# Tiles of a chunked gated attention with a mixture of experts, laid out in multiples of 64 bytes

## The chip, the cores and the metric

The kernel runs on one core of a Trainium2 chip. The metric is the device time of one execution in microseconds (us), the median over several runs.

## The reference

Two parts, one after the other. The first is a gated linear attention: per head a 48 x 48 state is decayed by a gate row by row, takes in the outer product of k and v, and is read with q. The second gives the result to four experts, each of two matrix products with a ReLU between them, and adds their outputs weighted by normalised probabilities.

```python
# q, k, v, f_logit: (4, 8, 768, 48) float32
f = 1.0 / (1.0 + np.exp(-f_logit))
for t in range(S):
    state = f[:, :, t, :, None] * state + np.einsum('bhd,bhe->bhde', k[:, :, t], v[:, :, t])
    y[:, :, t] = np.einsum('bhd,bhde->bhe', q[:, :, t], state)
x = y.transpose(0, 2, 1, 3).reshape(3072, 384)
# domain_probs (3072, 4), w1 (4, 384, 1024), w2 (4, 1024, 384)
p = domain_probs / (domain_probs.sum(-1, keepdims=True) + 1e-09)
for e in range(4):
    h = np.maximum(x @ w1[e], 0.0)
    out += p[:, e:e + 1] * (h @ w2[e])
```

## The kernel before

The sequence of 768 positions is cut into six chunks of 128 (`C`, `T`). In a chunk the four batches (`B`) go through the attention one by one, positions on the partitions: the gate (L260, L264, on ACT), a cumulated sum on PE (L268), its exponentials (L288), the products of q and k with them (L296, on DVE or POOL), a transposition (on PE for the first batches, by a DMA transpose later), the scores (L320), their masking (L324, on DVE), the product with v (`pe_y`, L331 and L335), and the transposition of the result into `xT` (L360 on PE, or a DMA transpose). The state of a chunk is carried on in `Sf` and `Sb` (L348, L355, L356).

The experts work on the 512 rows of a chunk (four batches of 128): `mm_h` (L364) multiplies `w1` with `xT`, ReLU takes the result into `h` (L373 on DVE, L375 on ACT), `mm_o` (L379) multiplies `h` with `w2`, and `ev_o` (L386 to L390) weights it and adds it to `o`, which is stored (L394). For chunk 0 the experts begin with the rows of batches 0 and 1 (256 columns), then those of batches 2 and 3.

Inputs are loaded by SP (`load`, L232). A tile of `f`, `q`, `k` or `v` holds two batches; there are four tiles of each name, numbered by slots (f0 to f3). A row of a tile holds the heads one behind the other, 48 float32 each, so one load of one batch is 128 partitions x 8 pieces of 192 bytes, 192 KB. For chunk 0 each batch is loaded by itself, in this order:

```python
for i, x in enumerate("f0 k0 q0 f1 k1 q1 f2 f3 k2 q2 v0 k3 q3 v1 v2 v3".split()):
    add_load(0, x[0], int(x[1]), 1, -1000 + i)
```

The number here is the batch, not the slot: batches 0 and 1 go to the tiles of slot 0, batches 2 and 3 to those of slot 1. Between v of batch 0 and k of batch 3 stands the load of the probabilities (L247). The gate's load of chunk 1, batch 0, follows; later chunks are loaded in pairs of batches.

The weights are loaded by POOL (`load_w`, L239), cast from float32 to bfloat16 on the way, in eleven pieces: six of 768 KB read (`w1` of experts 0 and 1 and `w2` of expert 0, in halves), then five whole matrices. The first piece waits for the load of q of batch 3 in chunk 0, so that the weights do not take the transfers away from the first loads.

The order of all the work on each engine is fixed when the kernel is built: a planner (`Plan`) places every step by its priority, its dependences, its assumed cost on each engine and the number of slots of each tile. While PE has no expert work yet, matmuls on a constant tile (`busy`, L614) fill the gaps that the planner foresees.

Tiles are taken from three pools in on-chip memory: `const`, `wpool` and `wk`. A tile of `wk` gets its place when it is first used. Places follow one another, and every length is rounded up to a multiple of 32 bytes. Nearly all lengths are multiples of 64 bytes; `ones` (2 bytes in a partition), `ident32` and `psm` (96 each) and the eight `egs` (16 each) are not. In `const` only `pn` lies between `ident32` and `psm`, and the weights and `wk` come behind.

Of the kernel before, what the change touches and what calls it, by code (L numbers as in the profile page):

```python
# [8 lines left out]
FP32 = mybir.dt.float32  # L9
BF16 = mybir.dt.bfloat16  # L10
AF = mybir.ActivationFunctionType
# [91 lines left out]
def kernel(  # L103
# [11 lines left out]
    nc = tc.nc  # L115
    B, H, S, D = q.shape
    assert (B, H, S, D) == (4, 8, 768, 48)
    T = 128
    C = S // T
    HD = H * D  # L120
    NP = H // 2
    P2 = 64
    MP = P2 + D
# [9 lines left out]
    const = ctx.enter_context(tc.tile_pool(name="const", bufs=1))  # L133
# [15 lines left out]
    nc.gpsimd.tensor_copy(out=Ub, in_=U)  # L149
    ident = const.tile([T, T], BF16)  # L150
    make_identity(nc, ident)
    ones = const.tile([T, 1], BF16)
    nc.gpsimd.memset(ones, 1.0)
    pads = {}
    for nm, nb in (("gp", 2), ("qk", 2)):
# [3 lines left out]
    for i in range(rooms["e"]):  # L159
# [5 lines left out]
        out=mask01, in_=mask01, compare_op=ALU.is_ge, fill=0.0,  # L165
# [4 lines left out]
    Sb = []  # L170
# [3 lines left out]
        Sb.append(t)  # L174
    NR = B * C
    praw = const.tile([NR, T, E], FP32)
    ident32 = const.tile([NR, NR], FP32)
    nc.vector.tensor_copy(out=ident32, in_=ident[0:NR, 0:NR])
    pn = const.tile([T, E, NR], FP32)
    psm = const.tile([T, NR], FP32)  # L180
    w1_sb = wpool.tile([128, E, KD, F], BF16)
    w2_sb = wpool.tile([128, E, KF, Din], BF16)
    w1_r = moe_w1.rearrange("e (ko ki) f -> e ki ko f", ki=128)
# [3 lines left out]
    for nm, a in (("f", f_logit), ("q", q), ("k", k), ("v", v)):  # L187
# [2 lines left out]
    tiles = {}  # L190
    shapes = {
        "f": ([T, 2 * H, D], FP32), "q": ([T, 2 * H, D], FP32), "k": ([T, 2 * H, D], FP32), "v": ([T, 2 * H, D], FP32),
        "ex": ([T, 2 * H, D], FP32), "egs": ([128, NP], FP32), "vb": ([T, H, D], BF16),
        "QK": ([128, 2, NP, T], BF16), "AT": ([T, 2, NP, T], BF16), "yb": ([T, HD], BF16),
        "xT": ([128, KD, NT], BF16), "h": ([128, KF, NT], BF16), "o": ([128, Din], FP32),
        "cs": ([T, 512], FP32), "tp": ([128, 2, NP, T], BF16), "A": ([T, NP, T], FP32), "y": ([T, 512], FP32),
# [3 lines left out]
    def tl(kind, *key):  # L200

        if (kind, key) not in tiles:
            room = kind if kind in rooms else "ps_m" if kind in ("hp", "op", "pp") else "ps_t"
            slot = P.slot[(room, kind) + key if room.startswith("ps_") else (room,) + key]
            if room in ("gp", "qk", "e"):
                tiles[kind, key] = pads[room, slot]
            else:
                shape, dt = shapes[kind]
                pool = ps if room.startswith("ps_") else wk
                tiles[kind, key] = pool.tile(shape, dt, name=f"{room}{slot}")  # L210
        return tiles[kind, key]
# [61 lines left out]
    def e_part(c, b, j):  # L273

        e = tl("e", c, b)
        if j == 0 and c > 0:
            return e[:, 0:2 * NP * P2].rearrange("t (r d i) -> t i r d", r=2, i=NP)[:, :, :, 0:D]
        e = e[:, 2 * NP * P2:] if j else e[:, 0:HD]
        return e.rearrange("t (i r d) -> t i r d", d=D, r=2)

    def exps(c, b):
        cs = tl("cs", c, b)
        src = cs[:, 0:HD].rearrange("t (i r d) -> t i r d", r=2, d=D)
        for j in range(2):
            o, i = e_part(c, b, j), src
            if j == 0 and c > 0:
                o, i = (x.rearrange("t i r d -> t r i d") for x in (o, i))
            nc.scalar.activation(out=o, in_=i, func=AF.Exp, scale=1.0 if j else -1.0)  # L288
        if c == 0:
            nc.scalar.activation(out=tl("egs", c, b)[0:MP], in_=cs[0:MP, HD:HD + NP], func=AF.Exp, scale=-1.0)  # L290

    def dma_egs(c, b):
        nc.gpsimd.dma_start(out=tl("egs", c, b), in_=tl("e", c, b)[T - 1:T, 0:2 * NP * P2].rearrange("o (m i) -> o m i", i=NP))  # L293

    def product(c, b, j, eng):
        engines[eng].tensor_tensor(out=tl("qk", c, b)[:, j, :, 0:D].rearrange("t (i r) d -> t i r d", r=2),  # L296
# [51 lines left out]
            nc.vector.tensor_tensor(out=Sf[rows, b], in0=Sf[rows, b], in1=KV[rows, :, r, :], op=ALU.add)  # L348

    def state(c, b):  # L350
        egs, nb = tl("egs", c, b), Sb[(c + 1) % 2]
        for r in range(2):
            rows = slice(r * P2, r * P2 + D)
            eg = egs[rows, :].unsqueeze(2).broadcast_to([D, NP, D])
            nc.gpsimd.tensor_tensor(out=Sf[rows, b], in0=Sf[rows, b], in1=eg, op=ALU.mult)  # L355
            nc.gpsimd.tensor_copy(out=nb[rows, b, :, r * D:(r + 1) * D], in_=Sf[rows, b])  # L356
# [72 lines left out]
    def attention(c, slot, gran):  # L429
# [10 lines left out]
        for b in range(B):  # L440
# [5 lines left out]
            cs = P.add(f"cs {c}.{b}", {"PE": 0.17 if c else 0.36}, on(pe_cs), s(0),  # L446
                       deps=[G[b]], takes=[pt_("cs")], lag=0.2, frees=[("gp", c, half)])
            ex = P.add(f"exps {c}.{b}", {"ACT": 0.98 if c else 0.82}, on(exps), s(0) + 0.1, deps=[cs],
                       takes=[("e", c, b)] + ([("egs", c, b)] if c == 0 else []), frees=[pt_("cs")])
            GS.append(P.add(f"egs {c}.{b}", {"POOL": 0.8}, on(dma_egs), s(10), deps=[ex], takes=[("egs", c, b)],  # L450
                            frees=[("e", c, b)], lag=2.8) if c and more else None)
            pe = {"DVE": 0.47} if c == 0 and b == B - 1 else {"DVE": 0.47, "POOL": 1.36} if c == 0 else None
# [56 lines left out]
        for b in range(B if more else 0):  # L509
            on = lambda f, b=b: (lambda e: f(c, b))  # L510
            pt_ = lambda kind, b=b: ("ps_t", kind, c, b)
            s15 = slot(b, 15) if c else 2 + 2 * b
            kv = P.add(f"kv {c}.{b}", {"PE": 0.22}, on(pe_kv), s15, deps=[Y[b]] + (X[B - 1] if c == 0 else []),
                       takes=[pt_("KV")], frees=[("vb", c, b), ("qk", c, b)], lag=0.2)
            ek = P.add(f"ev_kv {c}.{b}", {"DVE": 0.74}, on(ev_kv), s15 + 0.1,
                       deps=[kv, kvdone.get((c - 1, b))], frees=[pt_("KV")])
            kvdone[c, b] = P.add(f"state {c}.{b}", {"POOL": 1.75}, on(state), s15 + 0.2,
                                 deps=[ek, GS[b]], frees=[("egs", c, b)])
# [130 lines left out]
```

## Time and profile before

| | |
|---|---|
| median of 5 runs | 300.46 us (300.15 to 301.05) |
| the profiled execution, its own time | 301.05 us |
| its span, first to last instruction | 299.3 us |
| PE busy (matmul) | 288.9 us, 97% |
| ACT, DVE, POOL busy | 176.4, 125.8, 105.5 us |
| read from HBM, written to it | 31.51 MB, 4.72 MB |
| packets of the queue that SP uses | 129348, 30.14 MB |

The page shows the span in 40 equal slices, one digit for each, in tenths of the slice that an engine was busy. PEclk is the share of TensorE's clock that was granted. The DMA line is the mean busy share of the 16 DMA engines. An answer about stretches of time gives, for each stretch, the busy time of each engine with the number of its instructions, the clock, the DMA share and the rate in GB/s. A line of the timeline gives start, length, engine, line and operation, and in brackets how long the engine was idle before and what ended that. The chain of waits is followed back from the last instruction: at each step to what released it.

### The profile page before, as it was taken

The page shows a single profiled execution, that of the slowest core. Times are in us where ns is not written, and L with a number is a line of the kernel's source. Part 1 is how long each engine was busy: PE and PEld are TensorE (multiplying, and loading weights), DVE is VectorE, ACT ScalarE, POOL GpSimd, SP SyncE. Part 2 cuts the span into 40 slices and gives each one's busy share as a digit, 9 for nine tenths or more (in the row PEclk, how much of TensorE's full clock was granted, in tenths as well). Part 3 has the DMA queues.
Part 4 walks back from the last instruction along what each step waited for, and adds up shares of the span by engine and source line. Part 5 has one row for each costly group of instructions (what it writes and reads, how often), then busy time and mean ns, then how long its engine had stood idle before and what let it go on. Part 6 is the DMA issues. An engine that isn't in the chain of part 4 may idle for free.

```text
span 299.3 us, 5544 instructions
## 1 busy us (share of the span) xinstructions
PE 288.9 (97%) x2132; PEld 171.5 (57%) x2160; DVE 125.8 (42%) x247; ACT 176.4 (59%) x325; POOL 105.5 (35%) x179
## 2 busy tenths in 40 slices
PE   6879999999999999999999999999999999999995
PEld 2448555577777776455555555555555555555554
DVE  6656003486576475027374454433442322201223
ACT  4766672857766677876464665554465544475440
POOL 5376501229389159325538554234220000000000
PEclk9998999999999999999999999999999999999999
DMA  9999999996999999999999962102442100200003
GB/s 144 195 190 204 208 208 206 193 153 166 164 170 172 207 145 183 206 189 150 203 167 202 195 116 35 29 0 61 97 81 38 26 2 26 77 4 0 0 0 107
DMA packets 136462, 36.82 MB, mean 123 GB/s; under 512 B 126812, under 2 KB 135644, under 8 KB 136436
## 3 DMA queue, kind: packets, MB, share of 16 engines
q1 hardware_dynamic: 129348, 30.14, 59.9%
q0 software_dynamic: 7088, 6.33, 13.4%
q8 instruction: 17, 0.28, 0.4%
q14 instruction: 9, 0.07, 0.1%
HBM read 31.51 MB, written 4.72 MB: 121 GB/s over the span
## 4 chain that ended last, share of the span: by engine, by line
PE 91%; DMA 4%; SPq 4%; issue 1%; DVE 0%
PE ps_m L379 42%; PE ps_m L364 42%; SPq L232 3%; DMA w_sb<-in_moe_w_dram 2%; PE ps_t L320 2%; DMA q<-in_q_dram 1%; PE ps_t L335 1%; PE ps_t L331 1%; PE ps_t L341 1%; PE ps_t L268 1%; PE ps_t L305 0%; SPq L247 0%; PE ps_t L360 0%; DVE o L386 0%
## 5 line engine op out<-in xcount | busy, mean ns | idle before, releaser
L375 ACT ACTIVATE h<-ps_m 128x512 bf16<-128x512 f32 (+1 forms) x192 | 102.3, 538 | 91.3 <-PE ps_m L364 87.8
L364 PE MATMUL ps_m<-xT,w_sb 128*128 128x512 bf16 (+1 forms) x670 | 150.9, 343 | 1.5 <-DMA w_sb<-in_moe_w_dram 0.3
L379 PE MATMUL ps_m<-w_sb,h 128*128 128x384 bf16 (+1 forms) x776 | 151.6, 324 | 0.2
L379 PEld LDWEIGHTS <-h 128*128 128x128 bf16 x776 | 75.1, 98 | 58.6
L386 DVE SCALAR_TENSOR_TENSOR o<-ps_m,pn,o 128x384 f32<-128x384 f32 (+1 forms) x73 | 44.7, 613 | 110.3 <-PE ps_m L379 104.0
L364 PEld LDWEIGHTS <-w_sb 128*128 128x128 bf16 x696 | 66.0, 98 | 43.2 <-DMA w_sb<-in_moe_w_dram 0.4
L296 POOL TENSOR_TENSOR qk<-q,e 128x384 bf16<-128x384 f32 x19 | 22.5, 1191 | 34.9 <-ACT e L288 23.3
L324 DVE TENSOR_TENSOR AT<-ps_t,mask 128x512 bf16<-128x512 f32 x48 | 29.9, 682 | 5.4 <-PE ps_t L320 5.4
L355 POOL TENSOR_TENSOR Sf<-Sf,egs 48x192 f32<-48x192 f32 x40 | 20.0, 501 | 31.5 <-DVE Sf L348 29.4
L288 ACT ACTIVATE e<-ps_t 128x384 f32<-128x384 f32 x48 | 26.6, 667 | 4.0 <-PE ps_t L268 2.9
L373 DVE TENSOR_SCALAR h<-ps_m 128x256 bf16<-128x256 f32 (+1 forms) x40 | 20.0, 510 | 18.9 <-PE ps_m L364 16.7
L296 POOL TENSOR_TENSOR qk<-k,e 128x384 bf16<-128x384 f32 x20 | 20.2, 1010 | 9.0 <-ACT egs L290 4.8
L348 DVE TENSOR_TENSOR Sf<-Sf,ps_t 48x192 f32<-48x192 f32 x40 | 14.0, 350 | 10.9 <-PE ps_t L341 10.2
L239 POOL DMA_DIRECT2D w_sb<-in_moe_w_dram x11 | 9.0, 822 | 20.2 <-DMA k<-in_k_dram 16.4
L356 POOL CAST sb<-Sf 48x192 bf16<-48x192 f32 x40 | 13.5, 338 | 2.6
L388 ACT ACTIVATE o<-ps_m,pn 128x384 f32<-128x384 f32 x22 | 12.8, 580 | 2.8 <-PE ps_m L379 1.5
L335 PE MATMUL ps_t<-vb,AT 128*128 128x48 bf16 x192 | 11.6, 186 | 1.3 <-DVE vb L228 1.3
L228 POOL CAST vb<-v 128x384 bf16<-128x384 f32 x18 | 9.8, 563 | 8.5 <-DMA v<-in_v_dram 6.9
L260 ACT ACTIVATE ex<-f 128x768 f32<-128x768 f32 (+1 forms) x14 | 10.4, 746 | 3.9 <-DMA f<-in_f_logit_dram 3.9
L293 POOL DMA_DIRECT2D egs<-e x16 | 9.0, 563 | 10.4 <-ACT e L288 10.4
L614 PE MATMUL ps_m<-busy 128*128 128x512 bf16 x32 | 10.7, 434 | 1.6 <-DVE busy L144 1.5
L226 ACT CAST yb<-ps_t 128x384 bf16<-128x384 f32 (+1 forms) x16 | 7.5, 471 | 7.8 <-PE ps_t L335 7.7
(54 smaller groups left out, 123.2 us busy)
## 6 DMA issues: line engine op xcount, KB each, us to landing
out_dram<-o SPq DMA_DIRECT2D x23, 192.0 KB, 1.9
w_sb<-in_moe_w_dram POOLq DMA_DIRECT2D x5, 768.0 KB, 18.2
k<-in_k_dram SPq DMA_DIRECT2D x10, 384.0 KB, 5.6
q<-in_q_dram SPq DMA_DIRECT2D x10, 384.0 KB, 6.2
v<-in_v_dram SPq DMA_DIRECT2D x10, 384.0 KB, 5.9
f<-in_f_logit_dram SPq DMA_DIRECT2D x9, 384.0 KB, 4.9
w_sb<-in_moe_w_dram POOLq DMA_DIRECT2D x6, 384.0 KB, 9.1
f<-in_f_logit_dram SPq DMA_DIRECT2D x6, 192.0 KB, 4.4
```

The source lines that it names most:

```text
L288: nc.scalar.activation(out=o, in_=i, func=AF.Exp, scale=1.0 if j else -1.0)
L296: engines[eng].tensor_tensor(out=tl("qk", c, b)[:, j, :, 0:D].rearrange("t (i r) d -> t i r d", r=2), in0=tl("qk"[j], c, b // 2)[:, hh(b), ...
L324: nc.vector.tensor_tensor(out=tl("AT", c, b)[:, r].rearrange("s i t -> s (i t)"), in0=tl("A", c, b, r).rearrange("s i t -> s (i t)"), in1= ...
L335: nc.tensor.matmul(out=y[:, h * D:(h + 1) * D], lhsT=AT[:, r, i, :], rhs=vb[:, h, :], start=(c == 0), stop=True, skip_group_check=True)
L348: nc.vector.tensor_tensor(out=Sf[rows, b], in0=Sf[rows, b], in1=KV[rows, :, r, :], op=ALU.add)
L355: nc.gpsimd.tensor_tensor(out=Sf[rows, b], in0=Sf[rows, b], in1=eg, op=ALU.mult)
L356: nc.gpsimd.tensor_copy(out=nb[rows, b, :, r * D:(r + 1) * D], in_=Sf[rows, b])
L364: nc.tensor.matmul(out=tl("hp", c, e, fc, n0)[:, n0:n1], lhsT=w1_sb[:, e, kk, fc * 128:(fc + 1) * 128], rhs=tl("xT", c)[:, kk, n0:n1], sta ...
L373: nc.vector.tensor_relu(out=dst, in_=src)
L375: nc.scalar.activation(out=dst, in_=src, func=AF.Relu)
L379: nc.tensor.matmul(out=tl("op", c, e, nt, part)[:, cols], lhsT=tl("h", c, e, half_of(c, nt * T))[:, fc, nt * T:(nt + 1) * T], rhs=w2_sb[:, ...
L386: nc.vector.scalar_tensor_tensor(out=o, in0=op, scalar=pe, in1=o, op0=ALU.mult, op1=ALU.add)
```

## The change

Every tile of on-chip memory becomes a multiple of 64 bytes long. `ones` becomes 32 bfloat16 wide, `ident32` and `psm` 32 float32, `egs` 16 float32, and each use takes the slice that it took before. All later tiles then begin on a multiple of 64 bytes. No instruction, transfer or order is touched.

```diff
-    ones = const.tile([T, 1], BF16)
+    ones = const.tile([T, 32], BF16, name="ones")[:, 0:1]
...
-    ident32 = const.tile([NR, NR], FP32)
+    ident32 = const.tile([NR, 32], FP32, name="ident32")[:, 0:NR]
...
-    psm = const.tile([T, NR], FP32)
+    psm = const.tile([T, 32], FP32, name="psm")[:, 0:NR]
...
-        "ex": ([T, 2 * H, D], FP32), "egs": ([128, NP], FP32), "vb": ([T, H, D], BF16),
+        "ex": ([T, 2 * H, D], FP32), "egs": ([128, 16], FP32), "vb": ([T, H, D], BF16),
...
-            nc.scalar.activation(out=tl("egs", c, b)[0:MP], in_=cs[0:MP, HD:HD + NP], func=AF.Exp, scale=-1.0)
+            nc.scalar.activation(out=tl("egs", c, b)[0:MP, 0:NP], in_=cs[0:MP, HD:HD + NP], func=AF.Exp, scale=-1.0)
...
-        nc.gpsimd.dma_start(out=tl("egs", c, b), in_=tl("e", c, b)[T - 1:T, 0:2 * NP * P2].rearrange("o (m i) -> o m i", i=NP))
+        nc.gpsimd.dma_start(out=tl("egs", c, b)[:, 0:NP], in_=tl("e", c, b)[T - 1:T, 0:2 * NP * P2].rearrange("o (m i) -> o m i", i=NP))
...
-        egs, nb = tl("egs", c, b), Sb[(c + 1) % 2]
+        egs, nb = tl("egs", c, b)[:, 0:NP], Sb[(c + 1) % 2]
```

## The prediction

> **What bounds the kernel now.** I began with the page: where are PE and the DMA engines full, and what clock does PE get?
>
> ```profile
> span 299.3 us, 5544 instructions
> ...
> PE   6879999999999999999999999999999999999995
> ...
> PEclk9998999999999999999999999999999999999999
> DMA  9999999996999999999999962102442100200003
> ```
>
> A slice is 7.48 us. PE is full from the fourth slice to the last; the transfers are full from the start to about 172 us. So a faster transfer helps only where PE waits for one. The stretches tell where that is (the columns after the length are busy us of PE, PEld, DVE, ACT and POOL, then the granted clock, the DMA share and GB/s):
>
> ```profile
> 0.00:23.10 23.10, 17.24 (x161) 9.10 (x163) 13.90 (x33) 14.74 (x33) 12.67 (x26) 0.97 1.22 177
> 23.10:296.20 273.10, 271.66 (x1971) 162.44 (x1997) 111.44 (x213) 161.61 (x293) 92.88 (x154) 1.00 0.70 118
> ```
>
> From 23.1 us PE is idle for 1.4 us of 273. The end is therefore the moment at which the expert matmuls begin, plus a fixed length of PE work, plus 3.1 us of last store. What sets that beginning is in the chain of waits, asked for its first 26 us (start, length, what):
>
> ```profile
> 8.67 1.02 SPq L232
> ...
> 12.02 4.46 DMA q<-in_q_dram
> 16.49 0.30 issue
> 16.78 6.32 DMA w_sb<-in_moe_w_dram
> ...
> 23.14 2.10 PE ps_m L364 x9
> ```
>
> Nothing of an engine is in it. SP issues a load about every 1.0 us (L232) because the queue takes no more; the q load of batch 3 lands at 16.49; only then POOL issues the first weight piece, which lands at 23.10. Sixteen loads of 192 KB and one weight piece stand ahead of PE's long stretch.
>
> **What a 64-byte border is worth: the trace of before holds a sample.** The tiles lie one behind the other in order of first use, each length rounded up to 32 bytes. `ones` (32), `ident32` (96) and `psm` (96) make 224 bytes, three and a half times 64, so everything behind `psm` begins 32 bytes off a border: the weights, f0, k0, q0, ex0. egs0 takes 32 bytes and puts ex1 and f1 on a border; egs1 takes them off again (QK0, k1, q1, AT0, v0), egs2 on (QK1), egs3 off (v1 and the rest). Of the load tiles f1 alone is on a border now: it takes f of batches 2 and 3. Heads are 192 bytes apart, three times 64, so all rows of a tile share its phase. ACT's gate (L260) starts as f lands, after idle time:
>
> ```profile
> 3.92 0.52 ACT L260 ACTIVATE ex<-f 128x384 f32<-128x384 f32 x1 [1.83 <-DMA f<-in_f_logit_dram]
> ...
> 7.06 0.52 ACT L260 ACTIVATE ex<-f 128x384 f32<-128x384 f32 x1 [0.58 <-DMA f<-in_f_logit_dram]
> ...
> 10.05 0.52 ACT L260 ACTIVATE ex<-f 128x384 f32<-128x384 f32 x1 [0.42 <-DMA f<-in_f_logit_dram]
> ```
>
> Between the first two lie three loads off the border (k, q, f): 3.14 us, 1.05 each. Between the next two lie k and q off it and one f on it: 2.99. The load on the border took 0.90, 0.15 less. The rates of such stretches (same columns; the last is GB/s):
>
> ```profile
> 3.95:8.05 4.10, 2.43 (x16) 0.92 (x15) 1.95 (x4) 2.90 (x7) 1.00 (x1) 1.00 1.37 190
> 8.05:9.90 1.85, 1.71 (x16) 0.86 (x17) 1.02 (x2) 1.02 (x4) 0.26 (x1) 1.00 1.39 206
> ...
> 79.65:80.40 0.75, 0.75 (x7) 0.52 (x6) 0.39 (x1) 0.75 (x3) 0.54 (x1) 1.00 1.28 258
> ```
>
> The stretch in which f1 is filled moves 206 GB/s, the one ahead of it 190. The third is a load off the border, alone in the queue: 258. So being off the border costs something only while loads stand in line, as they do in the first 21 us.
>
> **The change part by part.** (a) Of the 14 loads up to q of batch 3, f1 takes two; the first, f0, and ten more gain: 11 x 0.15 = 1.65 us. That q lands at 14.84 in place of 16.49. (b) The first weight piece shares the engines with v of batches 1 to 3 and f of the next chunk, and lands behind them. Four loads of 1.05 and one piece of 1.92 (the next pieces land that far apart) make 6.12 us of the 6.61 from 16.49 to 23.10, so the engines lose only 0.49 there, and 4 x 0.15 = 0.60 is saved. The piece lands at 23.10 - 2.25 = 20.85. (c) Ahead of the first L364, PE's order has the y product of batch 3 (L335, ends at 22.84), which needs v of batch 3 (landed 20.76, 2.08 earlier). With three of those four loads ahead that v comes 1.65 + 0.45 = 2.10 earlier, and L335 ends at 20.74: just in time. (d) Engines that cover these waits: ACT is idle 0.42 before the gate at 10.05, which has to move by 6 x 0.15 = 0.90 while the gate at 7.06 moves by 0.60, so 0.12 of the cover is left. DVE has a y copy between the products of k and q of batch 3 and lets the q product move by 1.5; PE then has its 1.26 us of idle before L335 at 20.27. If one of these gave way, the beginning would move by 0.1 to 0.2 less.
>
> (e) The clock. PE had 0.50 from 21.92 to 25.33:
>
> ```profile
> 21.92:23.10 1.18, 0.92 (x12) 0.51 (x9) 0.00 (x0) 0.78 (x3) 1.18 (x2) 0.50 1.25 208
> 23.10:25.33 2.23, 2.19 (x12) 1.63 (x13) 0.72 (x2) 0.63 (x3) 0.85 (x3) 0.50 1.23 204
> ```
>
> This costs (25.33 - 23.14)/2 = 1.1 us of matmuls. If it stays where it is, L364 begins before it and pays for all 3.41 us: 1.7, a loss of 0.6. If it is gone, little more is won, because the sixth weight piece becomes late: it lands at 32.7 (issued 20.79, 11.9 to landing), and PE, whose first L379 group starts at 32.23 with four matmuls of 0.65 together, wants it at 32.88. That is 0.17 us of slack, and the piece moves by 2.25 as the first does. So the clock makes -2.25 into -1.65 at one end and -2.4 at the other; I take a quarter of the loss, 0.15. The Trainium skill ("TensorE: Matmul & The Clock Gate", Part 1) calls this window 3413 ns long and free-running, not restarted by a kernel; the trace's 3.41 us agrees, and by that rule its place changes from run to run, before and after alike.
>
> (f) Later loads go faster too, and nothing waits for them: PE's 1.4 us of idle in 273 covers all. The weights go on to a border as well; a piece takes 1.92 us for 768 KB read, half as much written. I cost that at nothing: the trace has no weight row on a border; by the f1 stretch it could be up to 8% (206 against 190), 0.15 a piece, a further gain for the first one alone. The widened ones, ident32, psm and egs keep their slices, 16-byte rows and counts; there are 352 more bytes in a partition, and no instruction, DMA or wait more. Last store: 3.1 us after PE, rows of 768 bytes; nothing, within 0.05.
>
> Sum: -1.65 - 0.60 + 0.15 = -2.1 us. The profiled execution was 301.05 (span 299.3 and 1.75 around it), the highest of five and 0.59 above the median; it becomes 298.95, span 297.2. From the median: 300.46 - 2.1 = 298.4.
>
> A rule speaks against this size. The Trainium skill ("DMA: Bandwidth & Descriptors", How a descriptor splits into AXI transactions) counts beats of 32 bytes and reads that start at 256-byte borders: a row on any 32-byte border fills whole beats, and 64 is no border at all. By its counting, 192-byte rows at steps of 192 take 9 beats on average from a 64-byte border and 10 from 32 off; as an estimate from that page 10% of 1.05 is 0.10 a load, 1.6 us in all, if it holds for the side that writes SBUF. It is not seen in rows of the trace whether it does; the sum goes by the 0.15.
>
> **The rivals.** *Less than the sample.* Two loads between others are a thin sample; if 0.07 is right, 15 x 0.07 = 1.05: 299.4. For it: v of batch 0 started ACT's cast at 14.23, 4.18 after the gate at 10.05, where 0.90 + 3 x 1.05 = 4.05 was due, so a load can miss by 0.13. *More.* Once all rows are on borders the queue may near the lone pace: 192 KB at 258 GB/s are 0.76 us, 0.29 less, 15 x 0.29 = 4.35. With 0.12 left at ACT I take 0.21, 3.1 in all: 297.3. *Nothing.* f1 was fast for another reason (its place in the queue): 300.46. Against it: the f load into f0 at 7.06, also behind a q, was not fast. *Slower, by PE's operands.* Every stationary and moving operand in SBUF moves by 32 bytes too. If that cost each of the 1971 matmuls behind 23.1 us 2 ns (1% of 203 to 217), 3.9 us are lost: 302.3. It decides from 2.1/1971 = 1.1 ns. Against it: QK1 is on a border now, QK0, QK2 and QK3 are not, and all 192 L320 matmuls took 212 to 227 ns, median 216. The gate reading f1 takes the same 0.52 us as from f0.
>
> **How the numbers follow.** The sample's price, 0.12 to 0.18 a load, with the clock's two ends: 1.8 - 0.6 to 2.7 + 0.17, so 297.6 to 299.3, 74 in 100. Less: 9 (one of them within 0.2%). More: 6. Nothing: 7. Slower: 4. About 0.2%, 0.6 us, is what a measurement of this kernel can tell from no change. Faster 0.88, same 0.08, slower 0.04. The range 297.4 to 299.7 holds the first case, most of the second and part of the third.
>
> **What would show it.** Right: ACT's gates still 3.9 first, then steps of about 2.7 where 3.14 and 2.99 were; 205 GB/s or more up to 8 us; POOL's weight issue near 15.1; the first L364 near 20.9; as little idle PE behind it. Wrong: steps of 3.1 (nothing); the same early L364 but L364 or L379 above 343 or 324 ns (operands); a PE gap near 30 us before L379 (the sixth piece); a half clock across the first L364, which takes back up to 0.6.

## The result, and the profile after

The changed kernel takes 299.24 us (median of 26 runs, 298.56 to 300.75); the kernel before took 300.46 in 47 runs beside it (300.08 to 302.34). The ratio is 0.9955, with a 95% interval of 0.9945 to 0.9964: faster by 1.2 us of medians, 1.35 by the ratio (1.1 to 1.7 by its interval), where 2.1 was forecast. Ratios leave out runs that are more than 1.5% above the fastest run of their kernel. The profiled execution had an own time of 298.69 us.

The page after, the same lines as before and with them the queue that SP uses (packets, MB, share of 16 engines):

```profile
span 297.0 us, 5544 instructions
...
PE   7989999999999999999999999999999999999995
...
PEclk9999999999999999999999999999999999999999
DMA  8999999997979999996989952102432100200003
...
q1 hardware_dynamic: 129348, 30.14, 52.0%
```

The clock is full in all slices. The queue carries the same packets and bytes as before, and they occupied 52.0% of the engines' time where they had occupied 59.9%: the mean packet is shorter. The two stretches, cut where the expert matmuls begin, first of before, then of after (columns as in the prediction):

```profile
0.00:23.14 23.14, 17.24 (x161) 9.10 (x163) 13.90 (x33) 14.78 (x33) 12.71 (x26) 0.97 1.22 177
23.14:296.18 273.04, 271.66 (x1971) 162.44 (x1997) 111.44 (x213) 161.57 (x293) 92.84 (x154) 1.00 0.70 118
...
0.00:21.39 21.39, 17.82 (x162) 9.71 (x164) 14.64 (x34) 14.55 (x33) 12.40 (x26) 1.00 1.00 186
21.39:293.89 272.50, 270.79 (x1971) 161.74 (x1997) 111.54 (x213) 161.16 (x292) 92.92 (x154) 1.00 0.64 119
```

The first is 1.75 us shorter (21.39 against 23.14). In the second PE is busy 0.87 less (270.79 against 271.66), as the half clock of the profile before is gone, and idle 0.33 more (1.71 against 1.38). Together 2.29 us, between the two profiled executions. The chain of waits, at its turn from the loads to the weights:

```profile
11.35 3.58 DMA q<-in_q_dram
14.93 0.30 issue
15.23 6.12 DMA w_sb<-in_moe_w_dram
21.34 0.05 issue
21.39 0.84 PE ps_m L364 x6
...
23.18 0.19 DVE psm L255
```

The same steps as before: q of batch 3 lands 1.56 us earlier, POOL issues at 15.23, the first weight piece lands 1.76 earlier. New is the L255 of DVE: PE waits 0.34 us for it at 23.04, a wait that neither profile of before has. ACT's gates:

```profile
3.79 0.52 ACT L260 ACTIVATE ex<-f 128x384 f32<-128x384 f32 x1 [1.71 <-DMA f<-in_f_logit_dram]
...
6.44 0.52 ACT L260 ACTIVATE ex<-f 128x384 f32<-128x384 f32 x1
...
9.80 0.54 ACT L260 ACTIVATE ex<-f 128x384 f32<-128x384 f32 x1
```

The gates at 6.44 and 9.80 no longer show a wait for a landing: ACT came to them straight from its own exponentials. The ones ahead of 9.80 waited for PE until 8.99, while f had landed at 9.34. So the pace is read from the landings in the trace: from 3.77 for f of batch 0 and 5.63 for q of batch 0 to 14.93 for q of batch 3, they lie about 0.9 us apart.

### The profile page after: what moved, and what is told of

Same layout as the page of the kernel before. It is cut to its first block, busy times and chain, and to the rows that moved or that the text cites. A ratio compares the mean times of both kernels' runs of the same rounds, so it can differ in the third digit from the quotient of the medians.

```text
span 297.0 us, 5544 instructions
## 1 busy us (share of the span) xinstructions
PE 288.6 (97%) x2132; PEld 171.5 (58%) x2160; DVE 126.6 (43%) x247; ACT 175.7 (59%) x325; POOL 105.3 (35%) x179
## 4 chain that ended last, share of the span: by engine, by line
PE 91%; SPq 3%; DMA 3%; issue 1%; DVE 1%
PE ps_m L379 42%; PE ps_m L364 41%; SPq L232 3%; DMA w_sb<-in_moe_w_dram 2%; PE ps_t L320 2%; PE ps_t L335 1%; PE ps_t L331 1%; DMA q<-in_q_dram 1%; PE ps_t L341 1%; PE ps_t L268 1%; PE ps_t L305 0%; SPq L247 0%; DVE h L373 0%; DVE o L386 0%; PE ps_t L360 0%
## 5 line engine op out<-in xcount | busy, mean ns | idle before, releaser
L364 PE MATMUL ps_m<-xT,w_sb 128*128 128x512 bf16 (+1 forms) x670 | 150.1, 341 | 2.3 <-DMA w_sb<-in_moe_w_dram 0.8
L379 PE MATMUL ps_m<-w_sb,h 128*128 128x384 bf16 (+1 forms) x776 | 151.7, 324 | 0.2
L379 PEld LDWEIGHTS <-h 128*128 128x128 bf16 x776 | 75.1, 98 | 58.6
L364 PEld LDWEIGHTS <-w_sb 128*128 128x128 bf16 x696 | 65.5, 98 | 43.9 <-DMA w_sb<-in_moe_w_dram 1.5
L373 DVE TENSOR_SCALAR h<-ps_m 128x256 bf16<-128x256 f32 (+1 forms) x40 | 20.0, 510 | 18.8 <-PE ps_m L364 16.6
L614 PE MATMUL ps_m<-busy 128*128 128x512 bf16 x32 | 11.8, 473 | 1.6 <-DVE busy L144 1.5
L335 PE MATMUL ps_t<-vb,AT 128*128 128x48 bf16 x192 | 11.5, 184 | 0.0
```

Of the source, the lines that this page charges most:

```text
L335: nc.tensor.matmul(out=y[:, h * D:(h + 1) * D], lhsT=AT[:, r, i, :], rhs=vb[:, h, :], start=(c == 0), stop=True, skip_group_check=True)
L364: nc.tensor.matmul(out=tl("hp", c, e, fc, n0)[:, n0:n1], lhsT=w1_sb[:, e, kk, fc * 128:(fc + 1) * 128], rhs=tl("xT", c)[:, kk, n0:n1], sta ...
L373: nc.vector.tensor_relu(out=dst, in_=src)
L379: nc.tensor.matmul(out=tl("op", c, e, nt, part)[:, cols], lhsT=tl("h", c, e, half_of(c, nt * T))[:, fc, nt * T:(nt + 1) * T], rhs=w2_sb[:, ...
```

## The experiments

Kernels that were measured together ran on one chip, beside runs of the kernel before. "Lands" is a landing in the trace, "first h" the start of the first L364 (L368 or L371 where lines have shifted), "gap" the longest wait of PE just after it (for the second weight piece, but in the first profile of after for L255).

| kernel | q of batch 3 lands | first weight piece: issued, lands | first h | gap | ratio to before, 95% |
|---|---|---|---|---|---|
| before, profiled execution | 16.49 | 16.78, 23.10 | 23.14 | - | 1 |
| before again | 16.50 | 16.79, 23.65 | 23.70 | 0.23 | 0.9979 (0.9958 to 1.0001) |
| after, profiled execution | 14.93 | 15.23, 21.34 | 21.39 | 0.34 | 0.9955 (0.9945 to 0.9964) |
| after again | 14.82 | 15.12, 21.66 | 21.71 | 0.78 | 0.9952 (0.9937 to 0.9966) |
| all tiles off | 16.89 | 17.19, 23.22 | 23.27 | 0.62 | 1.0011 (0.9995 to 1.0027) |
| only loads on | 15.60 | 15.89, 21.84 | 21.89 | 0.88 | 0.9956 (0.9938 to 0.9975) |
| only loads off | 16.77 | 17.07, 23.43 | 23.48 | 0.27 | 1.0017 (0.9998 to 1.0036) |

**Which tiles matter.** Four kernels: both originals once more, and the change divided between the tiles of the loads and everything else.

Before again has no edit.

> The kernel before, unchanged, for a second profile and the granted clock of every run. Theory (the profile of before had a half clock from 21.9 to 25.3 us that most runs do not have, so it overstates the gain): runs of 301 us and more show a clock of 0.993 to 0.996, runs of 300.1 to 300.5 a clock of 0.998 to 1.000; a profile at full clock begins L364 at about 23.1 and ends its span near 298.5. Rival (the spread has another source, in the transfers): the clock does not follow the time, and the first L364 begins at different times.

After again has none either.

> The changed kernel, unchanged, beside e6 and e7 on one chip, for a second profile. Theory (two things vary from run to run and not the loads: how long the first two weight pieces take behind their issue, and a DMA transpose into xT near 118 us): gates again 3.8, 6.4 to 6.7, 9.6 to 9.8, q of batch 3 at 14.9 to 15.6; the first L364 between 21.3 and 22.0; ratio 0.9945 to 0.997. Rival (the first profile of the changed kernel was an outlier at the loads too): q of batch 3 behind 16, gates 3 us apart.

All off takes back one tile, which puts everything behind it 32 bytes off. In the kernel that ran, `ident32` and `psm` keep their new lengths; the place of the later tiles is the one that the text on record means.

```diff
-    ones = const.tile([T, 32], BF16, name="ones")[:, 0:1]
+    ones = const.tile([T, 1], BF16, name="ones")
```

> egs takes 64 bytes, but ones, ident32 and psm keep their old lengths (224 bytes together), so every tile behind them, f1 and the weights too, begins 32 bytes off a 64-byte border. Theory (the border of the load tiles sets the pace of loads in line): the two loads into f1 lose their 0.15 us each, ACT's gates at 3.9, 7.06 and then 10.2 instead of 10.05; q of batch 3 lands at about 16.8; time 300.46 + 0.3 = 300.75, ratio 1.001. Rival (f1 was fast for its place in the queue): the gate stays at 10.05 and the ratio is 1.000 with q landing at 16.5.

Loads on adds 32 bytes inside the tiles of the loads alone, and so brings them back to a border while weights and products stay off. Loads off is the same lines in the changed kernel: only the loads leave the border.

```diff
-                tiles[kind, key] = pool.tile(shape, dt, name=f"{room}{slot}")
+                if kind in "fqkv":
+                    t = pool.tile([T, 2 * H * D + 16], FP32, name=f"{room}{slot}")
+                    tiles[kind, key] = t[:, 8:8 + 2 * H * D].rearrange("t (h d) -> t h d", d=D)
...
```

> As e1, but the f, q, k and v tiles are 64 bytes longer and their data begin 32 bytes in, so the loads alone are on 64-byte borders; weights, const tiles and all other work tiles are 32 off. Theory (the loads alone carry the gain): like the changed kernel, ratio 0.995 to 0.9965, q of batch 3 lands near 14.9, first L364 near 21.4. Rival (the weights' rows or the operands of the engines on borders carry part of it): ratio 0.997 to 1.000, with q landing early and the first weight piece or the matmuls later than in the changed kernel.

> The changed kernel with the data of the f, q, k and v tiles 32 bytes in: all tiles on 64-byte borders but the loads. Theory: as e1, ratio 1.001, q of batch 3 at about 16.8, three loads between gates 3.14 us. Rival (weights or operands carry part): ratio 0.997 to 0.999, with weight pieces landing less than 1.9 us apart or L364 and L379 below 343 and 324 ns.

With the loads on, alone, the whole gain is there (0.9956); with the loads off, alone, nothing is left of it (1.0017), whatever weights, products and PE's operands do. The measure is good to about 0.2%: before again against the other runs of the same kernel gives 0.9979. The profile with only the loads on has q of batch 3 at 15.60, where 14.9 was expected, and so 0.9 us of the 1.6; why its loads were slower than those of after is not known. The rival of PE's operands falls here too: one L364 took 341 ns in the profile before again, in all off and in the profile after, one L379 324. (The 343 of the first profile holds its half clock.) All off takes the border from f1 as well, two loads more: q of batch 3 lands 0.40 later than in before (0.3 was expected), which is too little to be seen in the time (1.0011).

The two repeats say how far one profile carries. Before again began at 23.70 with a full clock, after again at 21.71: 1.99 us, and PE ends 1.93 earlier (296.58 against 294.65). What was expected of before again, a beginning near 23.1 at full clock, did not come: its first weight piece took 6.86 us from issue to landing, where the first profile has 6.32.

**What a border is.** A kernel of loads alone: sixteen groups of eight loads, every load 128 partitions x 8 rows, with the length of a row, the step from row to row and the place of the first row changed from group to group. It leaves out the whole computation and stores zeros.

```python
for n, (row, step, off) in enumerate(cases):
    for i in range(8):
        dst = tiles[i][:, o:o + 8 * s].rearrange("t (h x) -> t h x", x=s)[:, :, 0:w]
        nc.sync.dma_start(out=dst, in_=src)
```

> Leaves out the whole computation and stores zeros. It times loads alone: sixteen groups of eight loads, 128 partitions x 8 rows, one behind the other on SP's queue, with rows of 192 bytes at steps of 192 or 256, of 256 at 256, of 512 at 512, the first row 0, 16, 32, 48, 64, 128 or 160 bytes behind a 256-byte border. Theory (writes into on-chip memory go in 64-byte pieces and a piece that is not whole costs like a whole one or more): 192 at 192 takes 0.90 us a load at 0 and 64, 1.05 at 16, 32 and 48; 192 at 256 is as fast at 0, 64 and 128, slow at 32 and 160; 256 is as fast at 64 and 128 as at 0, slower at 32; 512 loses at 32 by half as much in share. Rival (transactions begin at 256-byte borders, so a row costs by its place there): 192 at 256 takes 6 beats at 0, 7 at 32, 8 at 64, 10 at 128, 11 at 160, so 128 is nearly as slow as 160 and slower than 32.

The mean time from one landing to the next in a group, in us; the place counts from a border of 256 bytes. The loads of the next group already run beside the last of each:

| row, step in bytes | place: us per load |
|---|---|
| 192, 192 | 0: 1.02 (the first group); 16: 1.09; 32: 1.05; 48: 1.06; 64: 0.84 |
| 192, 256 | 0: 0.96; 32: 0.93; 64: 0.88; 128: 1.21; 160: 1.16 |
| 256, 256 | 0: 0.92; 32: 1.20; 64: 1.205; 128: 1.23 |
| 512, 512 | 0: 1.58; 32: 1.79 |

In the five slow groups at steps of 256 the single steps lie mostly at 1.18 to 1.22, in the last group at 1.81; the fast groups of 192 in 256 scatter, from 0.74 to 1.29.

Stretches from the first to the last landing of five groups (length, DVE, POOL, clock, DMA share, GB/s; a share over 1 means that packets overlap in time): 192-byte rows at steps of 192, places 32 and 64; then at steps of 256, places 32 and 128; last 256-byte rows, place 32.

```profile
21.21:28.55 7.34, 0.00 (x0) 0.00 (x0) 1.00 1.45 185
37.89:43.77 5.88, 0.07 (x1) 0.00 (x0) 1.00 1.03 187
55.25:61.77 6.52, 0.20 (x3) 0.00 (x0) 1.00 1.07 209
70.08:78.52 8.44, 0.00 (x0) 0.00 (x0) 1.00 1.52 164
99.24:107.67 8.43, 0.00 (x0) 0.00 (x0) 1.00 1.39 218
```

Seven steps lie in each length. The third row is 32 bytes off any border of 64 and is not slow (6.52); the fourth is on such a border and is the slowest (8.44). What they differ in is whether a row crosses a multiple of 256: in the third none does, in the fourth each does. The fifth writes 256 bytes in each row where the fourth writes 192, in the same time, since each row touches two blocks of 256 in both. With 512 bytes from place 32 it is three blocks: 1.81. So the theory on record, pieces of 64 bytes, falls, and of its rival the border of 256 holds. Where blocks set the pace, a load costs 0.60 us per block, or, if its 1024 rows lie evenly on 16 engines, 9.4 ns per row and block. This gives the number off the border at steps of 192: from 16, 32 or 48 off three quarters of the rows cross, 0.25 x 0.60 + 0.75 x 1.205 = 1.05. From a border of 64, places 0, 64, 128 and 192 take turns and half of the rows cross: 0.5 x 0.60 + 0.5 x 1.205 = 0.90. These are the 1.05 and 0.90 that the prediction read from the kernel before. But there is a floor: rows in one block don't reach 0.60 but stay at 0.88 to 0.96, with a DMA share of 1.07 where the crossing rows have 1.4 to 1.5, and 512 bytes in two blocks take 1.58, not 1.205. The half-crossing rows (0.84, share 1.03) look like those at the floor, so that their 0.90 need not be the sum. What sets the floor stays open.

One rival is left: a border at every 512 bytes with twice the price of a crossing. In every group above the floor just half as many rows cross one, so these times don't part the two. Borders of 64 and of 128 are out: rows of 192 at steps of 256 touch two pieces of 128 and three of 64 from place 64 (0.88) as from place 128 (1.21). And the prices are those of loads in line: the row of before at 79.65 us, which the prediction shows, moves rows that are 32 off a border at 258 GB/s, 0.76 us a load by that rate, under the price of their blocks and under the floor. Why a load can do so for 0.75 us is not shown.

The Trainium skill ("DMA: Bandwidth & Descriptors", How a descriptor splits into AXI transactions) has transactions start at 256-byte borders, which agrees, although here the reads of rows of one length are alike and the written side differs. It also counts beats of 32 bytes, and these rows do not follow the beats: by them place 64 would be a third dearer than place 0 (8 against 6) and 160 a tenth dearer than 128 (11 against 10); measured are 0.88 against 0.96, and 1.16 against 1.21.

**The same in the kernel.** To part the two borders where it counts, seven tiles of chunk 0's loads were laid out with heads 256 bytes apart, all else as in all off.

```diff
...
+    roomy = wpool.tile([T, 7 * 2 * H * 64 + 64], FP32, name="roomy")
+    for i, nm in enumerate(("f0", "k0", "q0", "f1", "k1", "q1", "v0")):
+        lo = 0 + i * 2 * H * 64
+        wide[nm] = roomy[:, lo:lo + 2 * H * 64].rearrange("t (h x) -> t h x", x=64)[:, :, 0:D]
...
```

With `lo = 0` rows begin 32 bytes behind a border of 256 and none crosses one:

> All tiles 32 bytes off a 64-byte border, as in e1; but the seven load tiles f0, f1, k0, k1, q0, q1 and v0 have their heads 256 bytes apart in place of 192, the first row 32 bytes behind a 256-byte border. So the rows of the loads into them are off every 64-byte border and none runs across a 256-byte border. Theory (a row costs by the number of 256-byte blocks that it touches, as e8 suggests): these loads go as fast as in the changed kernel, 0.90 us each: gates near 3.8, 6.5 and 9.2 to 9.8, q of batch 3 at 14.8 to 15.6, ratio 0.994 to 0.9965. Rival (64-byte borders): 1.05 each, gates 3.9, 7.05, 10.2, q of batch 3 at 16.8, ratio 1.001.

With `lo = 24` (96 bytes more) they begin 128 behind it, on a border of 64, and all cross:

> As e9, with the rows of these seven tiles 96 bytes later: 128 bytes behind a 256-byte border, so on a 64-byte border, and every row runs across a 256-byte border. Theory (256-byte blocks): 1.205 us a load as in e8, gates 3.6 us apart (4.0, 7.7, 11.3), q of batch 3 at 18.7, ratio 1.005 to 1.009. Rival (64-byte borders): as the changed kernel, ratio 0.9955, gates 2.7 to 3 us apart.

Off every border of 64, the first kernel is as fast as the change: 0.9956 (0.9942 to 0.997), q of batch 3 lands at 14.81. On a border of 64, the second is slower than the kernel before: 1.013 (1.0111 to 1.015), 304.51 us; q lands at 18.79. Its gates, in the timeline:

```profile
4.03 0.52 ACT L267 ACTIVATE ex<-roomy 128x384 f32<-128x384 f32 x1 [1.95 <-DMA roomy<-in_f_logit_dram]
...
7.71 0.52 ACT L267 ACTIVATE ex<-roomy 128x384 f32<-128x384 f32 x1 [0.95 <-DMA roomy<-in_f_logit_dram]
...
11.34 0.52 ACT L267 ACTIVATE ex<-roomy 128x384 f32<-128x384 f32 x1 [1.07 <-DMA roomy<-in_f_logit_dram]
```

Three loads each, 3.68 and 3.63 us: 1.2 a load, the price of two blocks. The packets of SP's queue occupied 64.3% of the engines' time, where before had 59.9 and after 52.0. The time is longer than the 1.005 to 1.009 expected: the expert matmuls begin at 24.74, only 1.0 later than in before again, but PE ends 3.1 later (299.71), as it also waits 0.74 for the second weight piece, 0.99 for a gate near 92 us and 0.58 for `xT` near 121.

**Where the rest of the 2.1 us went.** The first weight piece moved by 0.3 to 0.5 us less than forecast (1.76 and 1.99 in place of 2.25), and in after again the second made PE wait. Two places to look: the moment of POOL's issue, and the loads that still run beside the weights. The issue was moved ahead, to the landing of k of batch 3 and of v of batch 0.

```diff
-            after(ins["w", 0], ins[0, "q", B - 1])
+            after(ins["w", 0], ins[0, "k", B - 1])
```

The second kernel has `"v", 0` in the place of `"k", B - 1`.

> The changed kernel, but the first weight piece waits for k of batch 3 instead of q of batch 3, one load earlier; nothing else. Theory (2.3 us pass between POOL's issue and the first weight packet, and in the changed kernel the loads are nearly through by then, so the weights' start is what holds the experts): the issue moves from 15.23 to 14.4, the first packet to 16.7, the first piece lands near 20.6; the y product of batch 3 (L335) ended at 20.61 there and now follows v of batch 3 that shares with the weights a little earlier, so L364 begins at 20.7 to 21.2: 0.2 to 0.6 us less, ratio 0.993 to 0.995. Rival (total transfer work sets it): no change, as the loads behind take longer by what the weights gain, ratio as e5.

> The same with the first weight piece waiting for v of batch 0, two loads and the probabilities earlier than in the changed kernel. Theory: the issue at 13.1, the first packet at 15.4; now v of batches 1 to 3 share the engines with the weights and land later, v of batch 3 at 19.5 or later, and L335 with 1.8 us behind it makes the first L364 21.3 to 22: no gain over the changed kernel, ratio 0.995 to 0.998. Rival (the weights' start is still what holds): 0.9 us more than in e6, ratio 0.991.

One load earlier (issue 14.37), the first piece lands at 20.33 and L364 starts at 20.38, 1.0 earlier than after, and the time is the same: 0.9956 (0.9941 to 0.9972), as the rival had it. PE waits for later pieces instead:

```profile
PE ps_m L379 <- DMA w_sb<-in_moe_w_dram: 1.1, 1, 1.1
PE ps_m L364 <- DMA w_sb<-in_moe_w_dram: 0.7, 2, 0.5
```

The 1.1 is the fifth piece, the first of `w2`: it lands at 30.33, and PE has been ready for L379 since 29.28. (This fence and the next are the waits of PE between 20 and 36 us: total, times, longest.) Issued at 13.19 (after v of batch 0) the weights take the transfers from v: its batch 2 lands at 24.41 and its batch 3 at 30.26, where they were 18.34 and 18.77, and the kernel is 2.1% slower (1.021, 1.018 to 1.024), where 0.995 to 0.998 was expected. The profile is of the slowest of its six runs (310.64 us); how late v is in the others is not on record. PE waits in it for the product with v of batch 2, and then for ACT, which is held by its cast of v of batch 3:

```profile
PE ps_t L335 <- DVE vb L228: 6.1, 1, 6.1
PE ps_t L360 <- ACT yb L226: 4.7, 1, 4.7
```

The other place: the gate's load of chunk 1, batch 0, is the last of the early loads. In after again it was still running beside the second weight piece (landed at 24.41), and PE waited for that piece. Its lines in the timeline:

```profile
21.71 1.16 PE L364 MATMUL ps_m<-xT,w_sb 128*128 128x256 bf16 x9 [1.18 <-DMA w_sb<-in_moe_w_dram]
...
24.14 0.50 PE L364 MATMUL ps_m<-xT,w_sb 128*128 128x256 bf16 x3 [0.78 <-DMA w_sb<-in_moe_w_dram]
```

So that load was put together with the next one, for batch 1, which comes later; the order of the work on every engine stays as it was.

```diff
+        if (c, nm, b) == (1, "f", 0):
+            return
+        if (c, nm, b) == (1, "f", 1):
+            b, n = 0, 2
...
```

> The changed kernel, but the gate's load of chunk 1, batch 0 (192 KB, first used at 51 us) is not issued before the weights; it goes with that of batch 1 as one load of 384 KB, behind the eighth weight piece. All orders on the engines stay. Theory (in the changed kernel this load is the one that is still under way when the first two weight pieces stream, up to 24 us in e5, and delays them): the first weight piece lands at 20.9 to 21.3 and the second 1.95 behind it in every profile, PE waits less than 0.4 us between the first L364 and the first L379; ratio 0.992 to 0.9945. Rival (the weights' pace varies by itself): ratio as e5, 0.9952.

This is the fastest kernel of the study: 298.44 us (298.35 to 298.54, five runs), 0.9933 (0.992 to 0.9946), 0.6 less than the kernel with heads 256 bytes apart, which was measured beside it. Both weight pieces gain on after again:

```profile
21.15 1.16 PE L368 MATMUL ps_m<-xT,w_sb 128*128 128x256 bf16 x9 [0.84 <-DMA w_sb<-in_moe_w_dram]
...
23.09 0.50 PE L368 MATMUL ps_m<-xT,w_sb 128*128 128x256 bf16 x3 [0.29 <-DMA w_sb<-in_moe_w_dram]
```

The second lands 1.94 behind the first (2.43 in after again), and its wait is 0.29 in place of 0.78. Its five runs lie within 0.2 us, the 26 of the changed kernel within 2.2. The other profiles agree on the stray load: in the six in which it ran on for 0.7 us or more after the first weight piece had landed (all off, only loads on, after again, both earlier issues, rows from place 128), the second piece came 2.18 to 2.53 behind the first; in the five in which it did not (both of before, the first of after, only loads off, rows from place 32), 1.89 to 1.99. Both steps together, the late gate load and the early issue:

> e11 with the first weight piece waiting for k of batch 3, as in e6. Theory (with the gate's load of chunk 1 out of the way, the weights' start is what holds the experts, 2.3 us behind POOL's issue): the issue at 14.5, the first weight piece lands near 20.4, L364 begins at 20.5 to 20.9, the second piece lands 1.95 behind the first: 0.2 to 0.6 us less than e11, ratio 0.991 to 0.9927. Rival (v of batches 1 to 3 share the engines with the weights for longer and land later by what the weights gain): ratio as e11, 0.9933.

That failed: 0.9999 (0.997 to 1.0027), runs from 298.56 to 302.7. In the profiled one (302.37 us) k of batch 3 landed at 14.82 (14.08 in after), so that POOL issued at 15.12, not 14.5. Then v of batch 1 lands at 18.89 (15.90 in after), PE idles 1.56 us for it and has half its clock from 20.09 on; v of batch 3 lands at 22.19 (18.77 in after), and PE waits once more, 1.07. The stretches (as above, PE to POOL, clock, DMA share, GB/s):

```profile
18.00:20.09 2.09, 0.49 (x14) 0.47 (x15) 0.36 (x1) 1.18 (x3) 2.09 (x4) 1.00 1.12 167
20.09:26.92 6.83, 5.76 (x48) 3.70 (x45) 2.35 (x6) 3.32 (x9) 3.24 (x4) 0.50 1.24 205
```

Of its twelve runs eight had a mean clock of 0.994 or less (median 301.66), four a full one (298.99). The early issue alone does not explain the late v: with the issue at 14.37 and the gate's load in its old place, v of batch 3 had landed at 18.03. What does stays open.

## Why the prediction was right, and where it was off

The sign, the stage and the price of a load held; the sum was 0.7 to 0.9 us too large.

- **(a) Eleven loads x 0.15.** 1.65 was forecast, 1.56 measured between the two profiled executions (16.49 to 14.93) and 1.68 between the two repeats (16.50 to 14.82). The size held. The reason behind it was incomplete: "being off the border" of 64 bytes costs nothing in itself (the kernel with rows 32 behind a border of 256) and being on it gains nothing (place 128). Steps of 192 tie the two together, since they make half or three quarters of the rows cross a multiple of 256. The thin sample of f1 was good because it measured this layout itself.
- **(b) Four loads beside the first weight piece, 0.60.** This is the term that failed in size. From issue to landing the piece took 6.32 before and 6.12 after, 6.86 and 6.54 in the repeats: 0.2 to 0.3 won. The step took the engines for full all the time between, so that less work meant an earlier end. But POOL's piece has a start-up: its first packet comes 2.37 us after the issue before and 2.30 after (2.53 and 1.83 in the repeats). Faster loads leave engines unfilled in that time: between 16.5 and 19.1 us they moved 193 GB/s before, 176 after, 129 in after again. An earlier issue did bring the first piece 1.0 earlier, but the time it won was lost at later pieces.
- **(c) v and L335.** 20.74 forecast, 20.61 measured; still ahead of the first L364, now at 21.39.
- **(d) The covers.** ACT's 0.42 was used up, and the gate at 9.80 was late by 0.46 against its load. It did not reach the beginning of the expert matmuls, as (c) shows. DVE's L255 cost 0.34 in one profile, a wait that the prediction does not name.
- **(e) The clock.** Two errors. The piece named as late, the sixth, was not: it landed at 31.93, but L379 ran without a wait from 29.94 to 31.24, so PE's order calls on that piece later than 0.65 after the first L379. The late one is the second: 0.78 in after again, 0.88 with only the loads on. And the base held a half clock that most executions don't: of the 80 runs of before beside the experiments 10 had a mean clock of 0.995 or less, 7 of them among the 35 beside the divided kernels (median 301.72, 300.97 for the other 28), and of the changed kernel's none. The sum counted the clock as a loss of 0.15 and held its going to be worth no more than the 0.17 of the sixth piece; the profiled pair won 0.87 us of PE's busy time by it. So that pair moves by 2.36 (301.05 to 298.69), and the medians by 1.2.
- **(f) Weights and operands at nothing.** Held: only loads on gives 0.9956, the whole change 0.9952 to 0.9955.
- **The sum.** In the profiled pair the expert matmuls begin 1.75 earlier, PE is idle 0.33 more behind that, and the clock gives 0.87. Without the clock this is 1.42, inside the interval of the ratio. The 0.7 that the forecast of 2.1 has too much are then 0.1 in (a), 0.4 in (b) and 0.3 in new waits of PE close behind the first L364, which were put at nothing, less the 0.15 of the clock. The repeats, both at full clock, lie 1.93 apart at PE's end; the profiled run of before again was 0.7 above the median of its twelve (301.47 against 300.76), so one pair of profiles settles the split only roughly.

Of the rivals, *nothing* and *slower* fell by the divided kernels, and *more* by the landings, which stayed 0.9 apart. *Less than the sample* named nearly the time that came (299.4), but not for its reason: the price of a load was 0.15, as taken, and the loss came in (b) and in the new waits. That the time (299.24) fell into the stated range owes something to the range: it lies 0.8 above the 298.4 of the sum, near the upper end.

Two things stay open. Full-clock runs of before spread from 300.03 to 302.41, and the clock explains only part of the spread. Some profiles (before again, all off, loads off, and rows from place 128 a little later) have a wait of 0.3 to 1.1 us near 118.5 us for the transposing DMA of `yb` into `xT`, the first profile of before and those of the changed kernel do not:

```profile
PE ps_m L368 <- DMA xT<-yb: 1.1, 1, 1.1
```

This is the waits of PE between 100 and 130 us with only the loads off. Whether slower loads bring that wait on, or chance, was not tried.

## What to carry to other kernels

In these runs loads of many short rows, standing in line, were paid by the 256-byte blocks that its rows touch in on-chip memory, above a floor: lay rows out so that few cross, and look at the step as well as at the start. Where the trace already holds one instance of the changed state, its price carries further than a rule about the border. Time won in transfers is lost again if the next transfer has a start-up of its own or a stray load runs beside it; look at the second and third piece, not only at the first.

## What was not expected of the hardware

- A row of a load that touches two blocks of 256 bytes costs its engine 18.8 ns, with 192 bytes as with 256 (1.205 us per load of 1024 rows, if they lie evenly on 16 engines); in one block it costs about 14 to 15 (0.88 to 0.96 us).
- 1.6 to 2.5 us pass between POOL's issue of a casting weight load and its first packet.
- With the weights issued two loads earlier v of batch 3 landed 11.5 us later (30.26 in place of 18.77, in one profile), with the weights issued one load earlier 0.7 sooner (18.03): what the small rows in SP's queue lose against the weights in POOL's differed that much between these profiles.
- PE's half clock stood behind an idle PE: 0.50 from 20.09 to 26.92 us after 0.49 us of work in 2.09. That one brings on the other was not tried by itself.
